# The packed block's drive sums as two half-row sums over half of the tokens each, in groups of two pairs

## The chip, the cores and the metric

The kernel runs on one core of one Trainium2 chip. The metric is device time in microseconds (us). Each run also gives the span of its trace, from the first to the last instruction of the program that the trace holds; the time is some 1.9 us longer than that span.

## The reference

Layer norm, then a diagonal state-space recurrence times a gated feed-forward block. Cut to what matters (B = 1, L = 2048 tokens, D = P = 448, F = 1792, bfloat16):

```python
xn = _layernorm(x)
Bu = jnp.einsum("bld,pd->blp", xn + 0j, B_bar)      # the drive: complex, 448 states
for t in range(L):
    h = Lam_bar[None, :] * h + Bu[:, t, :]          # the recurrence
s = 2.0 * jnp.einsum("blp,dp->bld", hseq, Cmat).real + xn * Dskip
g = silu((silu(xn @ w_gate) * (xn @ w_up)) @ w_down)
return x + s * g
```

## The kernel before

Tokens go in four chunks of 512 (`W`). Chunk by chunk TensorE computes gate/up blocks (`gp`, `up`), the drive (`pb`, `pk`), the down projection (`hd`) and the output sum (`y`). ScalarE copies sums out of the eight banks of PSUM, the memory that TensorE writes its sums to. VectorE does norms, tables, the rotations and the scan.

448 is not a multiple of 128, so three whole blocks of 128 rows and one half block remain. A sum over 448 rows is therefore done as seven half-row (64-row) matmuls, and two such sums run at the same time, one in the upper and one in the lower row half, and then swap halves ("shares"). Going from 128-row to 64-row matmuls, or back, is called a change of row mode below. Between the shares a notice goes through GpSimd, so that the two halves do not write one bank at once.

The drive has 2 x 448 output states, in seven blocks of 128: three real, three imaginary, and one **packed** block with the last 64 of both. The three pairs run as concurrent half-row sums; the packed block had no partner, and was one whole sum of four 128-row matmuls. The whole sum takes block KF with its full 128 rows, half of which repeat rows of block 2, so `b_clear` zeroes those weights.

```python
    HALVES = (
        ([(0, H1), (1, H1), (2, H1), (KF, H1)], [(0, H2), (1, H2), (KF, H2)]),
        ([(0, H2), (1, H2), (2, H2), (KF, H2)], [(0, H1), (1, H1), (2, H1)]),
    )
...
    def tell(mm):

        told = nc.gpsimd.nop(nofuse=True)
        tc.add_manual_dep(told.ins, mm.ins.name, SYNC, reason="share")
        return told.ins.name

    def told_of(mm, notice):
        tc.add_manual_dep(mm.ins, notice, SYNC, reason="other half")

    def sums(banks, weights, q, c0, c1, between=None, told=None):

        left = []
        for share, first in ((0, True), (1, False)):
            for n in range(len(banks)):
                for m in range(4 - share):
                    for half in range(2):
                        i = half ^ share
                        d, h = HALVES[i][share][m]
                        mm = nc.tensor.matmul(
                            banks[n][i][:, c0:c1], lhsT=weights[n][i][h, d, :],
                            rhs=xT[h, d, q * W + c0 : q * W + c1],
                            start=(first and m == 0), stop=(not first and m == 3 - share),
                        )
                        if not first and m == 0:
                            told_of(mm, left[n])
                if first:
                    left.append(tell(mm))
                    if told:
                        told()
                        told = None
            if first:
                run_power()
            if first and between:
                between()

    def bu(q, ns, packed=None):

        pk = bank("pk") if packed == "first" else None
        pb = [[bank("pb") for _ in range(2)] for _ in ns]
        pk = bank("pk") if packed and pk is None else pk

        def whole():
            for d in range(KT):
                nc.tensor.matmul(
                    pk, lhsT=BT[:, d, block(KF)], rhs=xT[:, d, q * W : (q + 1) * W],
                    start=(d == 0), stop=(d == KF),
                )

        pairs = [[BT[:, :, block(n)], BT[:, :, block(KT + n)]] for n in ns]
        if packed == "first":
            whole()
        sums(pb, pairs, q, 0, W, between=whole if packed == "between" else None)
        if packed == "last":
            whole()
        for n, two in zip(ns, pb):
            for c in range(2):
                nc.scalar.activation(bu_of[q][c][:, n, :], two[c][:], ACT.Copy)
        if packed:
            b0, b1 = bu_of[q]
            nc.scalar.activation(b0[:, KF, :], pk[:], ACT.Copy)
            turn_over(b1[:, KF, :], pk)

    def turn_over(out, in_):

        for a, b in ((slice(0, R), slice(R, P)), (slice(R, P), slice(0, R))):
            nc.scalar.activation(out[a], in_[b], ACT.Copy)
...
    gu(0, bg, 2.0, {
        0: [*stats(4, 5, 6, 7), *sqrt(1), on(params_in), on(table_phase, 0)],
        1: [*bs(1), on(b_clear), *rstd_of(1), *norms(4, 5, 6, 7), on(table_sin, 0)],
        2: [*transposes(4, 5, 6, 7), on(load_c), on(table_phase, 1), on(table_sin, 1),
            on(bu, 0, (0, 1)), on(table_phase, 2), on(table_sin, 2)],
        3: [on(bu, 0, (2,), "between"), on(table_phase, 3), on(table_sin, 3), on(params_fold)],
        4: [on(params_trig), on(ssm_steps, bg, 0)],
        5: [on(params_out)],
    }, begun)
...
    def drive(q, packed, budget):
        bu_alloc(q)
        bu(q, (0, 1, 2), packed)
        ssm_steps(bg, q)
        bg.run(budget)

    drive(1, "last", 4.8)          # chunks 2 and 3: "first"
```

`table_sin(k)` is two ScalarE instructions (a sine and a cosine of 512 phases that VectorE has prepared). `gs` and `us`, which the gate/up copies write, have two buffers each, freed by the product `Vt` on VectorE.

## Time and profile before

| | before |
|---|---|
| time, first three runs | 190.18 us (190.11 to 190.31) |
| span of the profiled run (a slower one, 190.72) | 188.9 us |
| TensorE, VectorE, ScalarE busy | 97%, 85%, 55% |
| TensorE's share of the chain that ended last | 94% |
| four whole packed matmuls | 0.86 us, 0.97 after half-row matmuls |
| first gate/up matmul starts at | 7.85 us |

The page says that TensorE is the bound; the timelines say where it still stops. The prediction shows these lines. One thing about reading them: the time at which the first gate/up matmul starts depends on when the first input lands, and moved between 7.24 and 7.94 us over the profiled runs of all kernels here. Times of two traces are therefore compared **counted from that matmul**, and the tables below do so.

### The profile page before, as it was taken

How to read it: one execution, taken by the hardware profiler on the slowest of the kernel's cores; microseconds unless marked ns; L12 is line 12 of the kernel's file. 1: busy time of each engine (PE TensorE's matmuls, PEld its weight loads, DVE VectorE, ACT ScalarE, POOL GpSimd, SP SyncE). 2: the span in 40 equal slices, each digit the busy share in tenths (PEclk: the TensorE clock that was granted, in tenths of full speed). 3: DMA queues.
4: the chain of work that ended last, by engine and by line, in shares of the span. 5: the costliest groups of instructions: out<-in, count | busy, mean ns of one | idle time of the engine just before them, and what ended most of it. 6: DMA issues, size and time to landing. Idle time of an engine off the chain costs nothing.

```text
span 188.9 us, 3703 instructions
## 1 busy us (share of the span) xinstructions
PE 182.9 (97%) x1472; PEld 93.0 (49%) x1472; DVE 160.3 (85%) x267; ACT 104.0 (55%) x197; POOL 10.9 (6%) x21
## 2 busy tenths in 40 slices
PE   7799999999999999999999999999999999999992
PEld 3475434555555455544444455544444445555551
DVE  3889996799999999989999899789449999889253
ACT  3278599948999771107988632105996652302100
POOL 6422200000020000000020000000000000000000
PEclk9999999999999999999999999999999999999999
DMA  6999999100013100011005100020000000020020
GB/s 172 345 379 383 377 120 213 26 3 2 0 23 64 31 0 0 0 49 56 0 0 87 28 0 3 0 75 22 3 2 0 3 0 0 0 76 24 0 75 24
DMA packets 21121, 12.59 MB, mean 67 GB/s; under 512 B 11120, under 2 KB 20080, under 8 KB 21104
## 3 DMA queue, kind: packets, MB, share of 16 engines
q1 hardware_dynamic: 20288, 12.05, 24.3%
q10 hardware_dynamic: 688, 0.31, 0.6%
q8 instruction: 11, 0.18, 0.5%
q14 instruction: 6, 0.05, 0.1%
q0 software_dynamic: 128, 0.00, 0.0%
HBM read 8.03 MB, written 1.84 MB: 52 GB/s over the span
## 4 chain that ended last, share of the span: by engine, by line
PE 94%; DMA 2%; DVE 2%; ACT 0%; POOL 0%; issue 0%; SPq 0%; DVEq 0%
PE gp L428 24%; PE hd L567 23%; PE up L428 21%; PE y L582 11%; PE pb L428 10%; PE pk L453 2%; DMA x_all<-in_A_x_dram 2%; PE y L588 2%; PE tpb L371 1%; PE tp L259 1%; DVE ob L601 0%; DVE t L598 0%; DVE st L230 0%; ACT xT L261 0%; POOL sd L215 0%
## 5 line engine op out<-in xcount | busy, mean ns | idle before, releaser
L428 PE MATMUL gp<-xT,Wg 64*128 64x512 bf16 (+1 forms) x406 | 86.2, 369 | 0.1
L428 PE MATMUL up<-xT,Wu 64*128 64x512 bf16 (+1 forms) x406 | 85.9, 369 | 0.0
L428 PEld LDWEIGHTS <-Wg 64*128 64x128 bf16 x406 | 37.2, 94 | 23.8 <-issue 1.6
L428 PEld LDWEIGHTS <-Wu 64*128 64x128 bf16 x406 | 37.3, 94 | 19.5 <-POOLq L410 0.3
L567 PE MATMUL hd<-Wd,Vt 128*128 128x448 bf16 x224 | 43.2, 353 | 0.0
L554 ACT ACTIVATE gs<-gp 128x512 bf16<-128x512 f32 x56 | 35.1, 626 | 10.9 <-PE gp L428 7.5
L555 ACT ACTIVATE us<-up 128x512 bf16<-128x512 f32 x56 | 35.4, 633 | 0.0
L567 PEld LDWEIGHTS <-Vt 128*128 128x128 bf16 x224 | 21.8, 98 | 21.0 <-issue 0.8
L572 ACT ACTIVATE sg<-hd 128x448 bf16<-128x448 f32 x16 | 8.7, 543 | 38.3 <-PE hd L567 38.2
L559 DVE TENSOR_TENSOR Vt<-gs,us 128x2048 bf16<-128x2048 bf16 (+1 forms) x16 | 17.3, 1079 | 6.3 <-ACT us L555 6.3
L428 PE MATMUL pb<-xT,BT 64*128 64x512 bf16 x168 | 19.2, 376 | 0.0
L466 ACT ACTIVATE bu_re<-pb 128x512 bf16<-128x512 f32 x12 | 7.3, 611 | 20.9 <-PE pb L428 20.9
L598 DVE TENSOR_TENSOR t<-y,sg 128x448 f32<-128x448 f32 (+2 forms) x17 | 10.1, 595 | 10.0 <-PE y L582 9.6
L582 PE MATMUL y<-C,H_re 128*128 128x448 bf16 (+2 forms) x68 | 17.6, 342 | 0.0
L504 DVE TENSOR_TENSOR_SCAN bu_re<-rcol,H_re,ere 128x512 bf16<-128x512 f32 x12 | 15.1, 1268 | 0.0
L588 PE MATMUL y<-Dd,xT 128*128 128x128 bf16 x64 | 13.5, 212 | 0.0
L428 PEld LDWEIGHTS <-BT 64*128 64x128 bf16 x168 | 8.4, 94 | 10.1 <-issue 1.3
L582 PE MATMUL y<-C,H_im 128*128 128x448 bf16 (+2 forms) x51 | 11.9, 342 | 0.0
L230 DVE BATCH_NORM_STATS2 st<-x_all 128x6 f32<-128x448 bf16 x16 | 9.8, 616 | 2.0 <-DMA x_all<-in_A_x_dram 2.0
L504 DVE TENSOR_TENSOR_SCAN bu_im<-rcol,H_im,eim 128x512 bf16<-128x512 f32 x9 | 11.3, 1259 | 0.0
L601 DVE TENSOR_TENSOR ob<-t,x_all 128x448 bf16<-128x448 f32 (+2 forms) x17 | 10.2, 597 | 0.6
L215 POOL TENSOR_TENSOR sd<-vep,halves 128x1 bf16<-128x1 bf16 (+1 forms) x7 | 5.7, 813 | 77.8 <-PE up L428 41.8
(95 smaller groups left out, 174.9 us busy)
## 6 DMA issues: line engine op xcount, KB each, us to landing
out_dram<-ob SPq DMA_DIRECT2D x15, 112.0 KB, 1.7
Wd<-in_B_w_down_dram SPq DMA_DIRECT2D x1, 1568.0 KB, 12.0
x_all<-in_A_x_dram SPq DMA_DIRECT2D x1, 896.0 KB, 13.9
Wg<-in_B_w_gate_dram SPq DMA_DIRECT2D x1, 768.0 KB, 6.9
Wu<-in_B_w_up_dram SPq DMA_DIRECT2D x1, 768.0 KB, 8.2
x_all<-in_A_x_dram SPq DMA_DIRECT2D x1, 448.0 KB, 4.8
Wg<-in_B_w_gate_dram SPq DMA_DIRECT2D x1, 384.0 KB, 4.9
Wu<-in_B_w_up_dram SPq DMA_DIRECT2D x1, 384.0 KB, 5.3
```

The source lines that it names most:

```text
L230: nc.vector.bn_stats(out=st[:], in_=x_all[:, n, :])
L428: mm = nc.tensor.matmul(banks[n][i][:, c0:c1], lhsT=weights[n][i][h, d, :], rhs=xT[h, d, q * W + c0 : q * W + c1], start=(first and m == 0 ...
L504: nc.vector.tensor_tensor_scan(out=T["b"][c][:, k, :], data0=rcol[:, k : k + 1].to_broadcast([P, W]), data1=T["e"][c][:, k, :], initial=in ...
L554: nc.scalar.activation(gs[:, i + j, :], gp_[:], ACT.Silu)
L555: nc.scalar.activation(us[:, i + j, :], up_[:], ACT.Copy)
L559: nc.vector.tensor_tensor(out=Vt[:, f0 : f0 + n, :], in0=gs[:, 0:n, :], in1=us[:, 0:n, :], op=ALU.mult)
L567: nc.tensor.matmul(hd, lhsT=Vt_of[q][:, fi, j * P : (j + 1) * P], rhs=Wd[:, fi, :], start=(fi == 0), stop=(fi == NF - 1),)
L572: nc.scalar.activation(sg[:], hd, ACT.Silu)
L582: nc.tensor.matmul(y[:, c0:c1], lhsT=h, rhs=C2[:, n, c0:c1], start=(n == 0), stop=(n == NS - 1))
L588: nc.tensor.matmul(y[:, s + skip : s + P], lhsT=xT[:, n, m * P : (m + 1) * P], rhs=Dd[:, n, skip:P], start=False, stop=False,)
L598: nc.vector.tensor_tensor(out=t[:], in0=y, in1=sg[:, c0:c1], op=ALU.mult)
L601: nc.vector.tensor_tensor(out=ob[:], in0=t[:], in1=x_all[:, m, c0:c1], op=ALU.add)
```

## The change

The intent: let the packed block use the concurrent half-row form too. Its tokens are split into two halves of 256, and the two sums (same weights, other tokens) run in the two row halves. It saves TensorE time and, in chunk 0, two changes of row mode. As the half-row form takes each row once, the clear goes. The packed pair and the three others go in two groups of two pairs, so that at most four banks are open at once. The core of the diff (the rewritten argument lists of `sums` and `gu_matmuls` are cut):

```diff
-    def b_clear():
-
-        nc.vector.memset(BT[0 : P - R, KF, block(KF)], 0.0)
...
-    def bu(q, ns, packed=None):
-        pk = bank("pk") if packed == "first" else None
-        pb = [[bank("pb") for _ in range(2)] for _ in ns]
-        pk = bank("pk") if packed and pk is None else pk
-        def whole():
-            for d in range(KT):
-                nc.tensor.matmul(
-                    pk, lhsT=BT[:, d, block(KF)], rhs=xT[:, d, q * W : (q + 1) * W],
-                    start=(d == 0), stop=(d == KF),
-                )
...
-            nc.scalar.activation(b0[:, KF, :], pk[:], ACT.Copy)
-            turn_over(b1[:, KF, :], pk)
+    def bu(q, ns, packed=False):
+        C1 = W // 2
+        b0, b1 = bu_of[q]
+        ns = [*ns, KF] if packed else ns
+        for two in (ns[:2], ns[2:]):
+            pairs = []
+            for n in two:
+                pb = [bank("pb") for _ in range(2)]
+                if n < KF:
+                    pairs.append([(pb[i][:], BT[:, :, block(m)], (0, W))
+                                  for i, m in enumerate((n, KT + n))])
+                else:
+                    pairs.append([(pb[i][:, 0:C1], BT[:, :, block(KF)], (i * C1, i * C1 + C1))
+                                  for i in range(2)])
+            if pairs:
+                sums(q, pairs)
+            for n, pair in zip(two, pairs):
+                for i in range(2):
+                    to = bu_of[q][i][:, n, :] if n < KF else b0[:, KF, i * C1 : i * C1 + C1]
+                    nc.scalar.activation(to, pair[i][0], ACT.Copy)
         if packed:
-            b0, b1 = bu_of[q]
...
+            turn_over(b1[:, KF, :], b0[:, KF, :])
...
-        1: [*bs(1), on(b_clear), *rstd_of(1), *norms(4, 5, 6, 7), on(table_sin, 0)],
+        1: [*bs(1), *rstd_of(1), *norms(4, 5, 6, 7), on(table_sin, 0)],
...
-        3: [on(bu, 0, (2,), "between"), on(table_phase, 3), on(table_sin, 3), on(params_fold)],
+        3: [on(bu, 0, (2,), True), on(table_phase, 3), on(table_sin, 3), on(params_fold)],
```

More of the change, by code (lines that the diff above doesn't have):

```diff
@@ L415, in told_of, with sums @@
         tc.add_manual_dep(mm.ins, notice, SYNC, reason="other half")
-    def sums(banks, weights, q, c0, c1, between=None, told=None):
+    def sums(q, pairs, told=None):
         left = []
         for share, first in ((0, True), (1, False)):
-            for n in range(len(banks)):
+            for n, two in enumerate(pairs):
                 for m in range(4 - share):
                     for half in range(2):
-                        i = half ^ share
-                        d, h = HALVES[i][share][m]
+                        out, w, (c0, c1) = two[half ^ share]
+                        d, h = HALVES[half ^ share][share][m]
                         mm = nc.tensor.matmul(
-                            banks[n][i][:, c0:c1], lhsT=weights[n][i][h, d, :],
-                            rhs=xT[h, d, q * W + c0 : q * W + c1],
+                            out, lhsT=w[h, d, :], rhs=xT[h, d, q * W + c0 : q * W + c1],
                             start=(first and m == 0), stop=(not first and m == 3 - share),
@@ L441, in sums @@
                 run_power()
-            if first and between:
-                between()
-    def bu(q, ns, packed=None):
-        pk = bank("pk") if packed == "first" else None
-        pb = [[bank("pb") for _ in range(2)] for _ in ns]
-        pk = bank("pk") if packed and pk is None else pk
-        def whole():
-            for d in range(KT):
-                nc.tensor.matmul(
-                    pk, lhsT=BT[:, d, block(KF)], rhs=xT[:, d, q * W : (q + 1) * W],
-                    start=(d == 0), stop=(d == KF),
-                )
-        pairs = [[BT[:, :, block(n)], BT[:, :, block(KT + n)]] for n in ns]
-        if packed == "first":
-            whole()
-        sums(pb, pairs, q, 0, W, between=whole if packed == "between" else None)
-        if packed == "last":
-            whole()
-        for n, two in zip(ns, pb):
-            for c in range(2):
-                nc.scalar.activation(bu_of[q][c][:, n, :], two[c][:], ACT.Copy)
+    def bu(q, ns, packed=False):
[18 more added lines that the diff above has]
+                    nc.scalar.activation(to, pair[i][0], ACT.Copy)
         if packed:
-            b0, b1 = bu_of[q]
-            nc.scalar.activation(b0[:, KF, :], pk[:], ACT.Copy)
-            turn_over(b1[:, KF, :], pk)
+            turn_over(b1[:, KF, :], b0[:, KF, :])
     def turn_over(out, in_):
@@ L534, in gu_matmuls @@
     def gu_matmuls(q, f0, banks, c0, c1, **kw):
-        pairs = [[w[:, :, block(f)] for w in (Wg, Wu)] for f in (f0, f0 + 1)]
-        sums(banks, pairs, q, c0, c1, **kw)
+        sums(q, [
+            [(to[:, c0:c1], w[:, :, block(f0 + n)], (c0, c1)) for to, w in zip(two, (Wg, Wu))]
+            for n, two in enumerate(banks)
+        ], **kw)
     def gu(q, bg, budget, hooks={}, begun=None):
@@ L679, with drive @@
     })
-    def drive(q, packed, budget):
+    def drive(q, budget):
         bu_alloc(q)
-        bu(q, (0, 1, 2), packed)
+        bu(q, (0, 1, 2), True)
         ssm_steps(bg, q)
         bg.run(budget)
-    drive(1, "last", 4.8)
+    drive(1, 4.8)
     for q in range(NQ - 1):
@@ L696 @@
         if q + 2 < NQ:
-            drive(q + 2, "first", 4.0)
+            drive(q + 2, 4.0)
             n = (q + 3) * TQ
```

## The prediction

> **What bounds the kernel now.** I read the page first (busy shares, then the shares of the chain that ended last). TensorE is busy 97% and makes up 94% of that chain; VectorE (85%) and ScalarE (55%) follow.
>
> ```profile
> PE 182.9 (97%) x1472; PEld 93.0 (49%) x1472; DVE 160.3 (85%) x267; ACT 104.0 (55%) x197; POOL 10.9 (6%) x21
> PE 94%; DMA 2%; DVE 2%; ACT 0%; POOL 0%; issue 0%; SPq 0%; DVEq 0%
> ```
>
> Then the chain in order of time (columns: start us, us, what). The packed block's whole sum is `pk`, four matmuls in each of the four chunks; the other drive sums are `pb`.
>
> ```profile
> 26.21 0.86 PE pb L428 x8
> 27.07 0.97 PE pk L453 x4
> 28.04 0.75 PE pb L428 x6
> ...
> 64.11 0.97 PE pk L453 x4
> ...
> 81.75 0.86 PE pk L453 x4
> 82.61 4.64 PE pb L428 x42
> ```
>
> Four whole matmuls take 0.86 us, 0.216 each; it is 0.97 where 64-row matmuls stood before them, and the `pb` after them take 4.64 instead of the 4.53 that they take at 59.57. So a change of row mode costs 0.11 us. 42 `pb` in 4.53 us are 21 concurrent pairs of 0.216.
>
> The timeline of TensorE (start, us, engine, line, op) has the new form already, in the first gate/up block, which is summed over 256 columns at a time:
>
> ```profile
> 7.85 0.27 PE L428 MATMUL gp<-xT,Wg 64*128 64x256 bf16 x1
> 7.86 0.28 PE L428 MATMUL up<-xT,Wu 64*128 64x256 bf16 x1
> 7.96 0.27 PE L428 MATMUL gp<-xT,Wg 64*128 64x256 bf16 x1
> 8.07 0.27 PE L428 MATMUL gp<-xT,Wg 64*128 64x256 bf16 x1
> ```
>
> A pair of 256 columns takes 0.109 us (28 matmuls from 7.85 to 9.38), with no stop for the weight loads and none at 8.72, where the second shares wait for the notice through GpSimd.
>
> I then took every matmul's start and compared it with these steps. TensorE stands within 0.02 us per stage of that minimum from 46 us to the end, but for the mode changes. Before, in chunk 0, it stops at 34.98 (0.3 us), 35.95 (0.1) and 45.17 (0.15). Each follows by 0.05 us the end of a ScalarE copy out of a gate/up bank (34.93, 35.90, 45.12). So in chunk 0 ScalarE is the bound. Its timeline, with the idle time and releaser in brackets:
>
> ```profile
> 23.47 0.63 ACT L305 ACTIVATE ST<-f 128x512 bf16<-128x512 f32 x1 [1.84 <-DVE f L356]
> ...
> 28.34 0.62 ACT L555 ACTIVATE us<-up 128x512 bf16<-128x512 f32 x1
> ...
> 30.73 0.67 ACT L469 ACTIVATE bu_re<-pk 128x512 bf16<-128x512 f32 x1
> 31.41 1.19 ACT L475 ACTIVATE bu_im<-pk 64x512 bf16<-64x512 f32 x2
> 32.63 0.72 ACT L305 ACTIVATE ST<-f,two_pi 128x512 bf16<-128x512 f32 x1
> ```
>
> It has no gap from 23.47 to 39.9, and it started at 23.47 because VectorE's `f` was ready only at 23.44. VectorE's timeline:
>
> ```profile
> 17.61 0.61 DVE L379 COPY BT<-tpb 128x896 bf16<-128x896 bf16 x1
> 18.37 0.11 DVE L383 MEMSET BT<- 64x64 uint32 x1
> 18.41 0.14 DVE L240 RECIPROCAL rstd<-sd 128x4 f32<-128x4 bf16 x1
> ...
> 34.00 1.23 DVE L498 TENSOR_TENSOR ere<-bu_re,CT 128x2048 bf16<-128x2048 bf16 x1 [2.33 <-ACT CT L306]
> ...
> 41.74 1.22 DVE L559 TENSOR_TENSOR Vt<-gs,us 128x2048 bf16<-128x2048 bf16 x1
> ```
>
> It runs without a stop from 18.41 to 23.44, and again from 34.00 (released by ScalarE's last cosine, 33.97) to that `Vt`, which ends at 42.96. ScalarE writes the next `gs` at 43.05, since `gs` has two buffers and this `Vt` frees one (the profile puts the wait down to a matmul that was long done). Its fourth copy ends at 45.12 and frees the bank for 45.17. One chain thus goes from the clear at 18.37 through ScalarE and VectorE to TensorE at 45.17.
>
> **What the Trainium skill says.** "TensorE: Matmul & The Clock Gate", Back-to-back issue gap: a warm matmul of N columns costs N/2.4 + 2.5 ns, 216 for 512 and 109 for 256. The trace agrees for whole matmuls, and for pairs of 64-row ones (0.216, 0.109). "TensorEngine Tiling (Array Packing)", Key Properties: changing the tiling mode drains TensorE. The trace agrees: 0.11 us. "ScalarE: Activation LUTs", What ACT_TABLE_LOAD costs: an ACTIVATE with immediates takes 186 + 0.833 N ns, with overlap between neighbours. The trace has 0.58 to 0.66 us for 512 columns from PSUM (612 by the page), started every 0.48; the 256-column form does not occur, so I take 0.40 us and a step of 0.27 as an estimate from the page and that overlap.
>
> **The change part by part.**
>
> *TensorE, packed sum.* Removed per chunk: 4 x 0.216 = 0.86 us. Added: 14 half-row, half-width matmuls, 7 pairs x 0.109 = 0.76. Gain 0.10 per chunk, on the path: 0.30 for chunks 1 to 3.
>
> *TensorE, mode changes.* Chunk 0 had the whole sum between two shares: two changes, 0.2 us, both go. In chunk 1 (whole sum last, before `hd`) and chunks 2 and 3 (first, after `y`) there was one change, and one stays. So chunk 0 reaches the next gate/up block at 28.63 - 0.10 - 0.20 = 28.33 us.
>
> *Chunk 0, ScalarE.* Removed: `pk` copy 0.68 + two turned copies 1.22 = 1.90 us (30.73 to 32.63). Added: two 256-column copies, 0.27 + 0.40, then, as the turned ones now read their result, some 0.02 to 0.06 of wait, then two turned copies from SBUF at 0.64 each (their step at 97.8): 1.99. ScalarE's run gets 0.09 longer.
>
> *VectorE, the clear.* It waits for ScalarE's BT copy (ends 18.307), and holds VectorE from about 18.14 (independent instructions start 0.08 before their forerunner's end) to 18.41. Without it the reciprocal starts some 0.27 us sooner, and so do all steps up to `f`, and ScalarE's run from 23.47 on.
>
> *Sum for chunk 0.* ScalarE is 0.27 earlier before its packed copies and 0.18 after them. TensorE's earlier arrival is worth nothing: after the change all eight banks rotate strictly (the built program's bank numbers), and the block at 28.33 gets the banks of the block just before it, where before its first bank was one of `pb`'s. Its second bank is freed by the copy that ended at 28.965, now 28.70, so it starts at 28.75; the fourth at 29.72. That is a stop of 0.4 + 0.1 us, and the block ends at 31.87, against 31.65. The block at 34.98 finds its banks free at 34.89; its second half comes at 35.77 in place of 35.95. At 45.17 the chain gives 44.99. Net for chunk 0: -0.18 us.
>
> *Chunks 1 to 3, evacuation and banks.* The first four copies can start after 14 pairs (3.0 us) in place of 4.3, so ScalarE ends its drive copies about 1 us sooner. No matmul waits there, so it gains nothing. The tightest bank: the packed sum's second half in chunk 2 takes over `y`'s fourth bank, which VectorE frees at 85.11 (84.93 when its chain moves up); it is wanted at about 85.3. No stop, with 0.35 us to spare. Notices: the one for the third pair's first half now has the packed sum's four short steps and its own last one to pass, 4 x 0.109 + 0.216 = 0.65 us after its matmul starts; the 256-column case at 8.6 to 9.05 got along with 0.44.
>
> Total: -0.18 - 3 x 0.10 = -0.48; 190.18 - 0.48 = 189.70 us.
>
> **The rivals.**
>
> 1. *TensorE's sum alone decides*: 4 x 0.10 + 0.20 = 0.60 sooner, 189.58. Against it: the stops at 34.98, 35.95 and 45.17, fixed by ScalarE and VectorE.
> 2. *The chain in chunk 0 does not move up*: the clear is hidden, and only ScalarE's 0.09 counts. Then chunk 0 costs +0.09 and the total is -0.21: 189.97. For it: the reciprocal's 0.27 us is my inference from starts; another wait could take the clear's place.
> 3. *Strict rotation makes new waits*: the notice or a bank of `y` stops TensorE for 0.1 to 0.3 us in each drive, and the gain is gone: 190.2 or more. Against it: the room worked out above, and gate/up blocks of the same two-pair form run without a stop after 46 us.
> 4. *Short pairs are bound by weight loads* (two of 94 ns per 0.109 us): they would take 0.19 each, 1.3 us per sum, +0.45 us per chunk. Against it: the same form at 7.85 to 9.38.
>
> **Range and chances.** Between rival 1 and rival 2 lie 189.6 to 190.0; I lean to 189.7. Runs before differ by 0.2 us, and rival 3 could give back a few tenths: range 189.45 to 190.10. A change of 2% is 3.8 us, over six times everything that is touched, so within 2% is nearly certain.
>
> **What would show it.** In the profile after: matmuls 1472 + 40 = 1512; packed pairs 0.109 us apart with no step over 0.12; no mode change inside chunk 0's drive; ScalarE's first cosine-table instruction after its idle at 23.2 in place of 23.47; a stop of about 0.4 us at 28.3 to 28.75; stops at about 35.75 and 44.99; drives of chunks 1 to 3 each 0.10 shorter (5.40 us where it is 5.50 now, with the mode change). It would be wrong if a drive showed a stop at a bank or notice, or if ScalarE's run started at 23.47 as before.

## The result, and the profile after

The changed kernel takes **190.19 us** (190.17 to 190.19, 4 runs) against 190.25 (190.11 to 190.38, 4 runs) of the kernel before. The ratio is 0.9997, with a 95% interval of 0.9979 to 1.0014. Ratios here are the mean time of one kernel's runs over that of the other's of the same rounds, so not quite the ratio of the medians; the ratios of the later runs come out when one run of the kernel before, of 190.53 us, is left out. The forecast was 189.70; the time lies above its range.

The page of the changed kernel, busy shares and chain:

```profile
PE 182.1 (97%) x1512; PEld 93.9 (50%) x1512; DVE 160.3 (85%) x266; ACT 105.1 (56%) x201; POOL 11.2 (6%) x21
PE 84%; DVE 9%; ACT 3%; DMA 1%; issue 1%; POOL 0%; SPq 0%; DVEq 0%
```

TensorE has the 40 more matmuls. VectorE and ScalarE now have 12% of the chain, because the chain of chunk 0, told in the prediction, is followed in place of TensorE's own. The chain in order of time (start, us, what), at the drives of chunks 1, 2 and 3:

```profile
59.07 5.30 PE pb L424 x56
...
81.15 5.40 PE pb L424 x56
...
124.48 5.40 PE pb L424 x56
```

Where chunk 2's drive was 0.86 + 4.64 = 5.50 us it is 5.40, mode change included: 42 matmuls at 0.108 and 14 at 0.0545 are 5.30. The packed sum costs just what was worked out, and no matmul of a drive waits.

TensorE's timeline at the first gate/up block after chunk 0's drive (start, us, engine, line, op):

```profile
27.88 0.38 PE L424 MATMUL gp<-xT,Wg 64*128 64x512 bf16 x1
28.35 0.37 PE L424 MATMUL up<-xT,Wu 64*128 64x512 bf16 x1
...
29.33 0.37 PE L424 MATMUL up<-xT,Wu 64*128 64x512 bf16 x1
```

TensorE is there 0.30 us sooner than before (20.47 us after the first gate/up matmul; before 20.78), then waits until 28.35 for the bank that a copy frees at 28.30, and at 29.33 for the next. The two stops of the new bank order are there as forecast. ScalarE's timeline around them, with idle time and releaser in brackets:

```profile
22.80 0.63 ACT L305 ACTIVATE ST<-f 128x512 bf16<-128x512 f32 x1 [1.62 <-DVE f L356]
...
27.68 0.62 ACT L547 ACTIVATE us<-up 128x512 bf16<-128x512 f32 x1
...
30.06 0.73 ACT L458 ACTIVATE bu_re<-pb 128x256 bf16<-128x256 f32 x2
30.83 1.27 ACT L465 ACTIVATE bu_im<-bu_re 64x512 bf16<-64x512 bf16 x2
32.12 0.72 ACT L305 ACTIVATE ST<-f,two_pi 128x512 bf16<-128x512 f32 x1
```

From the first packed copy to the next table is 32.12 - 30.06 = 2.06 us, where it was 32.63 - 30.73 = 1.90. VectorE's timeline, where the clear was:

```profile
17.17 0.62 DVE L379 COPY BT<-tpb 128x896 bf16<-128x896 bf16 x1
17.70 0.17 DVE L240 RECIPROCAL rstd<-sd 128x4 f32<-128x4 bf16 x1
```

The reciprocal follows the copy's start by 0.53 us, before by 0.80. Counted from the first gate/up matmul, and in us:

| | before | after | difference |
|---|---|---|---|
| ScalarE's run starts (sine of table 1) | 15.62 | 15.40 | -0.22 |
| block after chunk 0's drive starts | 20.78 | 20.47 | -0.31 |
| chunk 0's rotation starts on VectorE | 26.15 | 26.09 | -0.06 |
| chunk 1's drive starts | 51.54 | 51.48 | -0.06 |
| `hd` of chunk 0 starts | 57.06 | 56.89 | -0.17 |
| gate/up of chunk 2 starts | 79.24 | 78.98 | -0.26 |
| gate/up of chunk 3 starts | 122.68 | 122.32 | -0.36 |
| end of the span | 181.01 | 180.65 | -0.36 |

So the trace gains 0.36 us, three quarters of what was forecast, and in the forecast places; but the time shows 0.06. The two profiled spans (188.9 and 188.1) cannot be compared as they stand, since the first one's input came 0.45 us later. What settled it is a number that the page does not have: **time less span**. It is 2.09 to 2.18 us in the changed kernel's four runs.

### The profile page after: what moved, and what is told of

Its sections match the earlier page's. It is cut to its first block, busy times and chain, and to the rows that moved or that the text cites. A ratio compares the mean times of both kernels' runs of the same rounds, so it can differ in the third digit from the quotient of the medians.

```text
span 188.1 us, 3787 instructions
## 1 busy us (share of the span) xinstructions
PE 182.1 (97%) x1512; PEld 93.9 (50%) x1512; DVE 160.3 (85%) x266; ACT 105.1 (56%) x201; POOL 11.2 (6%) x21
## 3 DMA queue, kind: packets, MB, share of 16 engines
q1 hardware_dynamic: 20288, 12.05, 23.2%
HBM read 8.03 MB, written 1.84 MB: 52 GB/s over the span
## 4 chain that ended last, share of the span: by engine, by line
PE 84%; DVE 9%; ACT 3%; DMA 1%; issue 1%; POOL 0%; SPq 0%; DVEq 0%
PE hd L559 23%; PE gp L424 20%; PE up L424 19%; PE y L574 11%; PE pb L424 9%; PE y L580 2%; DVE st L230 1%; DMA x_all<-in_A_x_dram 1%; DVE xn L248 1%; DVE f L356 1%; DVE a L357 1%; ACT CT L306 1%; DVE Vt L551 1%; ACT bu_im L458 1%; ACT bu_re L458 1%; DVE mv L231 1%
## 5 line engine op out<-in xcount | busy, mean ns | idle before, releaser
L424 PE MATMUL pb<-xT,BT 64*128 64x512 bf16 (+1 forms) x224 | 22.0, 349 | 0.0
L458 ACT ACTIVATE bu_re<-pb 128x512 bf16<-128x512 f32 (+1 forms) x20 | 10.0, 526 | 18.1 <-PE pb L424 18.1
L424 PEld LDWEIGHTS <-BT 64*128 64x128 bf16 x224 | 11.2, 94 | 11.0 <-issue 0.7
```

The costliest lines, as they stand in the source:

```text
L424: mm = nc.tensor.matmul(out, lhsT=w[h, d, :], rhs=xT[h, d, q * W + c0 : q * W + c1], start=(first and m == 0), stop=(not first and m == 3 ...
L458: nc.scalar.activation(to, pair[i][0], ACT.Copy)
```

## The experiments

Twelve runs, on one chip; they share their runs of the kernel before (11 in the end: time 190.11 to 190.56, span 188.2 to 188.7, time less span 1.82 to 1.92, mean 1.88). Spans are given to 0.1 us, so a single time less span is good to 0.05.

Two readings of the result had to be told apart. Theory A: both traces are right from the first gate/up matmul on, and the varying start hides the gain in the timed runs. Rival B: the time outside the traced span gives it back.

**Both kernels again.** No edit.

> The kernel before once more, for a second profile of it and five rounds against itself. Both theories expect a ratio of 1.000. Theory A (the change does save the 0.36 us that the two traces show from the first statistics on, and the runs hide it because the start varies): the first statistics on VectorE, which wait for the first input load, start at another time than 4.38 us, by up to 0.4, and the span differs from 188.9 by as much. Rival B (the time outside the traced span is what gives it back): they start near 4.38 again and the span is again 188.9.

Measured: 190.37 us (190.07 to 190.47), ratio 1.0008 (0.9996 to 1.0021); span from the first gate/up matmul 181.00, as before; time less span 1.83 to 1.87.

> The changed kernel once more. Theory A: 0.36 us under the kernel before of the same rounds (ratio 0.998), and a profile in which the packed drives are again 0.10 us shorter each and chunk 0 gains 0.05. Rival B: 0.06 us or less (ratio 0.9997), with the same profile from the first statistics on.

Measured: 190.15 us (190.01 to 190.30), ratio 1.0002 (0.9989 to 1.0015); span from the first gate/up matmul 180.61; time less span 2.11 to 2.25. Neither was right as written. The start does vary (first gate/up matmul at 7.61 and 7.24 us, where B expected it unchanged), but that does not hide the gain: the spans of the timed runs average 187.98 against 188.34 of the 11 runs of before, which is the 0.36 us of the traces. (The changed kernel's first four runs average 188.05. As the start varies from run to run, the agreement to 0.01 us is chance; what shows the gain is the two pairs of traces.) The gain is real inside the span, and B is right that it is given back outside: some 0.3 us more lie there in every run of the changed kernel.

**The clear put back** (its result is off).

```diff
+    def b_clear():
+        nc.vector.memset(BT[0 : P - R, KF, block(KF)], 0.0)
...
-        1: [*bs(1), *rstd_of(1), ...
+        1: [*bs(1), on(b_clear), *rstd_of(1), ...
```

> The changed kernel with the clear put back in its old place (its result is wrong on purpose: the clear now takes weights that the half sums use). If the clear held VectorE by 0.22 us in chunk 0, as the traces read, ScalarE's run starts 0.22 us later after the first statistics than in the changed kernel, and the first drive of chunk 1 starts 0.22 us later, so that the time is 0.14 us under the kernel before. If the clear was hidden, nothing moves against the changed kernel.

Measured: 189.98 us (189.93 to 190.22), ratio 0.9994 (0.9981 to 1.0006). ScalarE's run starts at 15.62 again, chunk 1's drive at 51.70, the end is at 180.85. VectorE's timeline shows the clear and what it holds up:

```profile
17.27 0.62 DVE L379 COPY BT<-tpb 128x896 bf16<-128x896 bf16 x1
18.03 0.11 DVE L383 MEMSET BT<- 64x64 uint32 x1
18.07 0.14 DVE L240 RECIPROCAL rstd<-sd 128x4 f32<-128x4 bf16 x1
```

The clear is thus worth 0.22 us of chunk 0, not hidden, and without its removal chunk 0 would lose 0.16 us to ScalarE's longer packed copies. But the point of the run is another: with the clear back, which costs time inside the span, time less span falls to 1.82 to 1.88, and the kernel gets no slower. Outside the span something follows the clear.

**Chunk 0 in the old form, chunks 1 to 3 changed** (wrong in chunks 1 to 3).

```diff
+        if packed and q == 0:
+            ...one pair, with whole() between the shares, pk copied and turned as before...
+            return
         ns = [*ns, KF] if packed else ns
```

> Chunk 0 as before (one whole packed sum between the shares, clear in place), chunks 1 to 3 as changed (their result is wrong on purpose because of the clear). If each changed drive saves its 0.10 us on the path: 0.31 us under the kernel before, and chunk 1's drive starts at the time after the first statistics that it has in the kernel before. If the drives give it back somewhere, less.

Measured: 190.06 us (189.88 to 190.61), ratio 1.0005 (0.9992 to 1.0019): the time alone says nothing, as this kernel's starts were spread widely (span 188.0 to 188.8). In the trace chunk 1's drive starts at 51.55 and the end is at 180.72, 0.29 us under before: 0.10 for each of the three drives. Time less span 1.81 to 1.88.

The theory now was that what lies outside the span follows VectorE's instruction stream, which is two built instructions shorter without the clear (314 in place of 316, counted in the built program, waits included: the clear, and a wait before it. The page counts 266 in place of 267, as waits are not busy).

**Two spare clears on VectorE**, in the changed kernel.

```diff
+    spare = ctile([P, 1], F32, "spare")
+    for _ in range(2):
+        nc.vector.memset(spare[:], 0.0)
     warm(11)
```

> The changed kernel with two tiny clears of an unused tile at its start on VectorE, while that waits for input: VectorE's instructions are then as many as before (the change took out the clear and a wait). Theory C (the changed kernel gains 0.37 us inside the traced span, and loses about 0.3 outside it, because VectorE's instruction stream is two instructions shorter): span as in the changed kernel, time less span back from 2.1 to 2.25 us to about 1.83, time 0.3 us under the kernel before. Rival D (what lies outside the span comes from something else in the change): time less span stays at 2.1 or more, time as in the kernel before.

Measured: 189.85 us (189.70 to 190.40, 6 runs), ratio 0.9988 (0.9975 to 1.0000). The trace from the first gate/up matmul is that of the changed kernel (end at 180.65); time less span is 1.82 to 1.90 in five runs and 2.30 in one.

**The kernel before without the clear**, nothing else (wrong).

```diff
-        1: [*bs(1), on(b_clear), *rstd_of(1), ...
+        1: [*bs(1), *rstd_of(1), ...
```

> The kernel before without the clear and nothing else (its packed sums are wrong on purpose). Inside the span: chunk 0's ScalarE run starts 0.22 us earlier after the first gate/up block, and the span is 0.2 us shorter. Theory C: time less span rises to about 2.1 us, so that the time is 0.1 us over the kernel before. Rival D (TensorE's longer stream or the GpSimd notices cause it): time less span stays at 1.83, time 0.2 us under the kernel before.

Measured: 190.34 us (190.20 to 190.56), ratio 1.0012 (0.9998 to 1.0025). Chunk 1's drive starts at 51.31 and the end is at 180.76, both some 0.24 earlier than before, and yet the time is no shorter: time less span is 2.10 to 2.16. TensorE's longer stream and the further notices are out: this kernel has neither.

**ScalarE relieved in chunk 0**, on the changed kernel and on the one before: the turned copies of chunk 0 go to VectorE, and block 2's sine and cosine after the drive's copies.

```diff
-        if packed:
+        if packed and q:
             turn_over(b1[:, KF, :], b0[:, KF, :])
+    def turn_on_vector():
+        b0, b1 = bu_of[0]
+        for a, b in ((slice(0, R), slice(R, P)), (slice(R, P), slice(0, R))):
+            nc.vector.tensor_copy(out=b1[a, KF, :], in_=b0[b, KF, :])
...
-            on(bu, 0, (0, 1)), on(table_phase, 2), on(table_sin, 2)],
-        3: [on(bu, 0, (2,), True), on(table_phase, 3), on(table_sin, 3), on(params_fold)],
-        4: [on(params_trig), on(ssm_steps, bg, 0)],
+            on(bu, 0, (0, 1)), on(table_phase, 2)],
+        3: [on(bu, 0, (2,), True), on(table_phase, 3), on(table_sin, 2), on(table_sin, 3), ...],
+        4: [on(turn_on_vector), on(params_trig), on(ssm_steps, bg, 0)],
```

> The changed kernel with ScalarE relieved in chunk 0: the two turned copies on VectorE, and the sine and cosine tables of block 2 after the drive's copies. If ScalarE's run is what ate TensorE's gain in chunk 0, there is no stop on TensorE between 28 and 46 us, and chunk 1's drive starts about 0.85 us earlier than in the kernel before, counted from the first gate/up block: 1.15 us under the kernel before in all, 189.0. If the bank order alone stops TensorE, a stop near 28.3 stays and the gain is 0.5 or less.

Measured: **189.19 us** (189.02 to 189.28), ratio 0.9949 (0.9935 to 0.9963). TensorE's, ScalarE's and VectorE's timelines of this kernel:

```profile
27.81 0.38 PE L424 MATMUL gp<-xT,Wg 64*128 64x512 bf16 x1
27.81 0.38 PE L424 MATMUL up<-xT,Wu 64*128 64x512 bf16 x1
28.03 0.38 PE L424 MATMUL gp<-xT,Wg 64*128 64x512 bf16 x1
```

```profile
28.86 0.74 ACT L458 ACTIVATE bu_re<-pb 128x256 bf16<-128x256 f32 x2
29.39 0.73 ACT L305 ACTIVATE ST<-f 128x512 bf16<-128x512 f32 x1
...
31.14 0.81 ACT L306 ACTIVATE CT<-a,half_pi 128x512 bf16<-128x512 f32 x1
```

```profile
30.97 0.59 DVE L466 COPY bu_im<-bu_re 64x512 bf16<-64x512 bf16 x2
31.98 1.22 DVE L494 TENSOR_TENSOR ere<-bu_re,CT 128x2048 bf16<-128x2048 bf16 x1 [0.42 <-ACT CT L306]
```

The stop at the bank is gone: both matmuls of the pair start at 27.81, the next pair 0.22 later. VectorE copies the two turned halves in 0.59 us, in time in which it had waited for the last cosine, where ScalarE took 1.27 in the changed kernel; its wait before the rotation is 0.42 in place of 2.33 (kernel before). TensorE's steps from there to chunk 1's drive add up to 0.03 us over the minimum (0.57 in the kernel before); that drive starts at 50.69, 0.85 sooner than before, and the end is at 179.82: 1.19 us under before. Time less span is 1.82 to 1.88 (316 built VectorE instructions). The edit has two parts, the turned copies and the later sine and cosine; no run has one without the other, so what each is worth is not shown.

> The kernel before with the same relief of ScalarE in chunk 0. If ScalarE's run alone held back TensorE there, the 0.55 us of stops go, and it is 0.55 us under the kernel before. The relieved changed kernel is then the whole 0.60 us of the packed sum under this one (0.10 in each of four chunks and 0.20 for two mode changes), where without relief only 0.37 was seen. If they are only 0.35 apart, chunk 0's gain is lost to something else.

Measured: 189.80 us (189.58 to 189.95), ratio 0.9982 (0.9969 to 0.9994). Chunk 1's drive at 51.00, the end at 180.43: 0.58 under before, the three stops. The relieved changed kernel is 180.43 - 179.82 = **0.61 us** shorter from the first gate/up matmul: with ScalarE out of the way the change is worth the whole 0.60 that TensorE's instructions add up to. (The medians of time are also 0.61 apart; in part by chance, as this kernel has 318 built VectorE instructions and a time less span of 1.88 to 2.05.)

**How far does VectorE's number go?** Four kernels with spare clears: two on GpSimd, one and four on VectorE, in the changed kernel; two on VectorE in the kernel before. The edit is the one above with another number or `nc.gpsimd`.

> The changed kernel with the two spare clears on GpSimd in place of VectorE. Theory C (what lies outside the traced span follows VectorE's own number of instructions): time less span stays at 2.1 to 2.25 us. Rival (any two more instructions mend it): it falls to 1.83.

> The changed kernel with one spare clear on VectorE (315 built instructions; 314 in the changed kernel, 316 before). Theory C with a threshold between 314 and 316: time less span is either 2.1 or more, or 1.83, and tells on which side 315 lies. If it grows evenly with the number, it is about 2.0.

> The changed kernel with four spare clears on VectorE (318). The relieved kernel before had 318 and 1.88 to 2.05 us outside its span. If VectorE's number alone sets it, about 2.0 here too; if more instructions are simply better, 1.83.

> The kernel before with two spare clears on VectorE (318). If VectorE's number alone sets what lies outside the span: about 2.0 us there, and 0.1 us over the kernel before in time, with the same span. If not, 1.83 to 1.9 and the same time.

Measured, with the earlier kernels, in order of VectorE's built instructions:

| VectorE | kernel | time less span, us | mean | median time |
|---|---|---|---|---|
| 314 | changed, first runs | 2.09 to 2.18 | 2.13 | 190.19 |
| 314 | changed, again | 2.11 to 2.25 | 2.19 | 190.15 |
| 314 | changed, two spare on GpSimd | 2.17 to 2.22 | 2.19 | 190.09 |
| 314 | before without the clear | 2.10 to 2.16 | 2.13 | 190.34 |
| 315 | changed, one spare | 1.74 to 1.88 | 1.78 | 189.82 |
| 316 | before (11 runs) | 1.82 to 1.92 | 1.88 | 190.15 |
| 316 | before, again | 1.83 to 1.87 | 1.85 | 190.37 |
| 316 | chunk 0 old, drives changed | 1.81 to 1.88 | 1.85 | 190.06 |
| 316 | changed, two spare | 1.82 to 1.90, one 2.30 | 1.93 | 189.85 |
| 316 | changed, clear back | 1.82 to 1.88 | 1.84 | 189.98 |
| 316 | changed, relieved | 1.82 to 1.88 | 1.84 | 189.19 |
| 318 | changed, four spare | 1.83 to 2.04 | 1.98 | 189.93 |
| 318 | before, two spare | 1.86 to 2.07 | 1.96 | 190.47 |
| 318 | before, relieved | 1.88 to 2.05 | 1.99 | 189.80 |

Ratios of the last four: 0.9998 (0.9985 to 1.0012) with two spare on GpSimd, 0.9988 (0.9974 to 1.0002) with one on VectorE, 0.9990 (0.9977 to 1.0004) with four, and 1.0018 (1.0005 to 1.0032) for before with two. That last one is 0.32 us over before in the medians, not 0.1, because its spans average 188.5 against 188.3: its trace ends at 181.01 from the first gate/up matmul, as before. By their means the kernels fall into groups by VectorE's number, whatever TensorE, ScalarE and GpSimd run; single runs of 316 and 318 overlap. It is neither even growth nor "more is better": 315 is the least, 314 the most, 318 between. Against 1.88 of before, the changed kernel pays 0.25 to 0.31 us outside its span, and 0.36 - 0.28 = 0.08 is what is left of its gain: the measured 0.06.

Why the number of VectorE's instructions shows there stays **open**. The trace holds nothing but transfers before its first and after its last program instruction, and the first and last instructions of the span look the same in all kernels. One trace of those transfers is of use: in each of the three kernels with 318, the records of the DMA queues hold one 8 KB transfer of an instruction queue (q14) that starts 1.74 to 2.00 us after the span's end, and none of the other eleven traces holds any transfer after the end. So with 318 something about fetching instructions differs after the end. Whether that transfer costs time is not shown, and between 314, 315 and 316 the traces show no such difference: for the 0.25 to 0.31 us of the change neither the side nor the mechanism can be read.

## Why the prediction was wrong

- **TensorE, packed sum: right.** 0.10 us per chunk was forecast; the three drives gave 0.11, 0.09 and 0.10 (differences of the table), and 0.29 together with chunk 0 left as it was.
- **TensorE, mode changes: right.** Chunk 0's next block starts 0.31 us sooner, against 0.30.
- **Banks and notices: right.** The two stops of the new bank order came at 20.95 and 21.93 us after the first gate/up matmul, forecast at 20.90 and 21.87 (28.75 and 29.72 less 7.85). No drive stops at a bank or a notice, so rival 3 is out; packed pairs run at 0.109 us, so rival 4 is out.
- **The bound in chunk 0: right, with two terms mis-sized.** The step "ScalarE's run gets 0.09 longer" measured 0.16: the 256-column copies took 0.46 and 0.47 us there, where 0.40 was estimated (over all chunks they average 0.414), and 2.06 in place of 1.99 in all. The step "the reciprocal starts some 0.27 us sooner ... and so do all steps" was right for the reciprocal (0.53 after the copy, 0.80 before), but that then took 0.17 in place of 0.14 us, and ScalarE's run moved by 0.22, which taking the clear out alone and putting it back both show. Together chunk 0 gave -0.06 where -0.18 was forecast. Rival 2 (the clear hidden) is out. Rival 3's time, 190.2, is close to what was measured, but by coincidence, since the stops that it rests on are not there; and rival 1 (TensorE's sum alone) holds only when ScalarE is relieved, where 0.61 was measured for its 0.60.
- **The failed step** is the last line of the sum, "190.18 - 0.48 = 189.70": it takes what happens in the trace off the time, as if the rest were constant. It is not: removing the clear, and with it two of VectorE's built instructions, added 0.25 to 0.31 us outside the span (taken out alone it did the same; two spare clears took it back). By what mechanism stays open. Inside the span the forecast of 0.48 met 0.36; had the rest stayed at 1.88, the time would have been 190.25 - 0.36 = 189.89, inside the range, as it is with two spare clears (189.85). Of the miss of 0.49 us some 0.28 is this term, 0.12 the two terms of chunk 0, and 0.07 the median of before, which was 190.25 in the runs compared and 190.18 in those the forecast started from.
- The forecast also put absolute times of a trace whose start was late (7.85 us) beside those to come; that cost nothing in the sum, but a reader of "28.75" must take the start off first. And the instruction at 23.47 that its last paragraph calls the first of a cosine table is the sine (`ST`); it came at 22.80, which is 23.25 on the old start, for 23.2 forecast.

## What to carry to other kernels

Pairing a sum without a partner with itself, over two halves of the moving data, gives the concurrent form to an odd block, and saved what the instructions add up to (here the eighth that had been padding, 0.10 us of 0.86); but a gain on the busiest engine counts only in stages where that engine sets the pace, so find the stage (here the first) where another engine frees its banks, and relieve that engine together with the change. Compare traces from a common event, not from their start. And where tenths of a microsecond matter, look at time less span as well: in this program an instruction taken out of VectorE's stream raised it, and one or two spare ones put in brought it back, for a reason that is still open.

## What the Trainium skill lacked or had wrong

- "TensorE: Matmul & The Clock Gate", Back-to-back issue gap: it puts whole 512-column matmuls in a stream of weight loads and matmuls at about 131 ns each and says that N/2.4 + 2.5 over-counts there, a caveat that the prediction left out. Here whole 512-column matmuls with a weight load each ran at 216 ns apart (0.86 us for four), just that formula. Neither that section nor the page's part on packing gives the spacing of a stream of concurrent 64-row pairs, which kept it too: 216 ns for 512 columns, 109 for 256, with two weight loads per pair hidden.
- "TensorEngine Tiling (Array Packing)", Key Properties: it names the drain at a change of mode without a size. Here it was 0.10 to 0.11 us each.
- "ScalarE: Activation LUTs", What ACT_TABLE_LOAD costs: its formula gives 399 ns for 256 columns; in a run without gaps the trace shows 462 and 471 (mean of all 414), started 264 ns apart. The formula is stated for 128 partitions; it would give 612 ns for the turned copies of 64 partitions, which took 628 from SBUF on ScalarE (VectorE took 0.59 us for two).
- No page tells that time outside the traced span goes with the number of VectorE's instructions, as it did here: 2.13 to 2.19 us for 314 of them, 1.78 for 315, 1.84 to 1.93 for 316, 1.96 to 1.99 for 318 (means).
